# The first layernorm of a two-layer transformer block: statistics first, two tiles normalised on ACT, x loaded on two queues

## The chip, the cores and the metric

The kernel runs on one core of one Trainium2 chip. The metric is the device time of one execution in microseconds (us). A lone core has no second die to compare with, so all timed runs below count as fast ones (the three single looks near the end have the state "unknown"); the granted TensorE clock, the share of full speed that the profiler records, was 0.998 to 1.0 over every whole run.

Engines are named as in the profile: PE is TensorE's matmul side, PEld its weight loads, DVE is VectorE, ACT is ScalarE, POOL is GpSimd, SP is SyncE, which here only issues DMAs.

## The reference

Two layers, each of a dilated sliding-window attention and a dense GELU block, with a layernorm without weights in front of each, over 2048 tokens of width 1024 in bf16:

```python
x = x + A(layernorm(x), wqkv, wo)      # 32 heads of 32; window of 8 keys, dilation 2
x = x + B(layernorm(x), w1, b1, w2, b2) # 1024 -> 3584, gelu, 3584 -> 1024
x = x + A(layernorm(x), wqkv, wo)
x = x + B(layernorm(x), w1, b1, w2, b2)

def layernorm(x):                       # eps 1e-5
    return (x - mean(x)) / sqrt(var(x) + eps)
```

## The kernel before

The kernel works on four groups of 512 tokens, each of four tiles of 128 tokens (`NTT = 4`). All x tiles stay in on-chip memory. What matters here is the head of the program: until the first group's four tiles are normalised, transposed and copied to `xnT`, PE has nothing real to do, because every QKV matmul of a group reads all 512 tokens of `xnT`.

```python
def load_x(g):
    for tt in range(NTT):
        t = g * NTT + tt
        sp.dma_start(x[t][:], x_in[t * P:(t + 1) * P, :])
...
def ln_stats(t):
    stats = lnp.tile([P, 2, 6], F32, name="stats")     # lnp: two buffers of each name
    for h in range(2):
        vec.bn_stats(stats[:, h, :], x[t][:, h * HALF:(h + 1) * HALF])
    mv = lnp.tile([P, 2], F32, name="mv")
    vec.bn_aggr(mv[:], stats[:])
    rstd = lnp.tile([P, 1], F32, name="rstd")
    pool.tensor_tensor(out=rstd[:], in0=mv[:, 1:2], in1=eps_t[:], op=ALU.add)
    pool.tensor_tensor(out=rstd[:], in0=rstd[:], in1=mhalf[:], op=ALU.pow)
    return mv, rstd

def ln_norm(t, mv, rstd):
    xn = lnp.tile([P, D], BF16, name="xn", bufs=3)
    vec.tensor_scalar(out=xn[:], in0=x[t][:], scalar1=mv[:, 0:1], scalar2=rstd[:], op0=ALU.subtract, op1=ALU.mult)
    return xn

def transpose_on_pe(xn, out):
    pst = psum.tile([P, KD, P], BF16, name="acc", bufs=6)
    for k in range(KD):
        pe(nc.tensor.transpose(pst[:, k, :], xn[:, k * P:(k + 1) * P], ident[:]))
    act.copy(out, pst[:])
...
def ln_first():
    ...
    s = [ln_stats(0)]
    for tt in range(NTT):
        if tt + 1 < NTT:
            s.append(ln_stats(tt + 1))
        xn = ln_norm(tt, *s[tt])
        transpose_on_pe(xn, xa[0][:, tt, :, :])
        warm_up(4)                      # four 512-column matmuls on zeros
...
warm_up(16)
ln_first()
build_constants()
...
    load_x(1)
    stage(gen_qkv(0, 2), ...)           # the real work begins
    ...
    stage(q2, 18)                       # Q, K and two of eight V chunks of group 2
    stage(gen_wo(0, 2))                 # then the output projection of group 0
```

In `ln_stats`, mv holds mean and variance of each token, and rstd is one over the standard deviation, which POOL computes from mv in two operations. `warm_up` is there to keep PE active, so that its clock is at full speed when the real matmuls come. A chunk is eight matmuls of PE, 1.73 us. The weights go through one pool of five 1 MB buffers (`wt`), so a weight load waits until PE is done with the tile five loads earlier.

## Time and profile before

| | before |
|---|---|
| median of 3 runs | 1247.13 us (1247.12 to 1247.34) |
| span of the profiled run | 1245.4 us |
| PE busy | 1232.9 us, 99% |
| first QKV matmul starts | 14.18 us |
| PE idle after that, in waits over 0.2 us (named ones) | 0.73, 0.5, 0.5, 0.2 us |

Two lines of the page of before; the first column is the engine's busy time, the second its share of the span:

```profile
PE 1232.9 (99%) x5757; PEld 627.9 (50%) x5807; DVE 836.5 (67%) x863; ACT 305.7 (25%) x475; POOL 97.7 (8%) x215
...
PEclk9999999999999999999999999999999999999999
```

PE is busy for 99% of the span at full clock, so time can be won only where PE does nothing or nothing useful. The timeline of PE in the first 45 us (start in us, duration, engine, line, operation, output and inputs, shapes, count; in brackets the idle time just before and what ended it) shows where that is:

```profile
1.05 4.91 PE L118 MATMUL acc<-big 128*128 128x512 bf16 x16 [1.05 <-DVE big L93]
6.89 0.62 PE L187 MATMUL acc<-ident,xn 128*128 128x128 bf16 x8 [0.93 <-POOL rstd L93]
...
12.37 0.61 PE L187 MATMUL acc<-ident,xn 128*128 128x128 bf16 x8
12.81 1.03 PE L118 MATMUL acc<-big 128*128 128x512 bf16 x4
14.18 26.06 PE L118 MATMUL acc<-xnT,wt 128*128 128x512 bf16 x120 [0.34 <-ACT xnT L93]
```

The matmuls on `big` are warm-up, those on `ident` are the transposes. From 14.18 us on, PE runs real matmuls back to back. DVE in the same stretch (before):

```profile
3.50 1.29 DVE L93 BATCH_NORM_STATS2 stats<-x 128x6 f32<-128x512 bf16 x2 [2.51 <-DMA x<-in_A_x_dram]
4.82 0.21 DVE L93 BATCH_NORM_AGGREGATE mv<-stats 128x2 f32<-128x12 f32 x1
4.95 1.23 DVE L93 BATCH_NORM_STATS2 stats<-x 128x6 f32<-128x512 bf16 x2
...
6.34 0.49 DVE L93 TENSOR_SCALAR xn<-x,mv,rstd 128x1024 bf16<-128x1024 bf16 x1
...
10.50 0.49 DVE L93 TENSOR_SCALAR xn<-x,mv,rstd 128x1024 bf16<-128x1024 bf16 x1
11.70 0.55 DVE L93 TENSOR_SCALAR xn<-x,mv,rstd 128x1024 bf16<-128x1024 bf16 x1 [0.71 <-PE acc L187]
```

DVE starts when the first x tile lands and goes on without a pause until 11.0 us; the last normalisation then waits 0.71 us. It waits for two things, a free `xn` buffer and rstd of its tile, and the line names PE, which reads the buffers.

In the waits of PE between 30 and 200 us (engine and line, what was waited for, us in total, times, longest):

```profile
PE acc L118 <- ACT vT L93: 0.7, 1, 0.7
```

That wait of 0.73 us ends at 100.41 us, where the Q matmuls of group 2 begin.

### The profile page before, as it was taken

What the parts mean: (1) busy time and instruction counts of PE and PEld (TensorE: products, weight loads), DVE (VectorE), ACT (ScalarE), POOL (GpSimd) and SP (SyncE); (2) the same over time, 40 slices, a digit from 0 to 9 for tenths busy, and PEclk for the clock granted to TensorE, in tenths of its full rate; (3) what the DMA queues carried; (4) which work ended last, traced back from release to release, by engine and by line L of the source; (5) the groups of instructions that cost most, each with busy time, mean ns of one, the idle gap of its engine ahead of it and who ended that gap; (6) DMA issues with size and microseconds to landing.
All of it is one profiled execution on the core that took longest, in us unless ns stands there. A gap on an engine that the chain in (4) does not pass through costs nothing.

```text
span 1245.4 us, 13928 instructions
## 1 busy us (share of the span) xinstructions
PE 1232.9 (99%) x5757; PEld 627.9 (50%) x5807; DVE 836.5 (67%) x863; ACT 305.7 (25%) x475; POOL 97.7 (8%) x215
## 2 busy tenths in 40 slices
PE   8999999999999999999999999999999999999998
PEld 5666544446444564445644456444654444444443
DVE  4999989896995999427993379943598786011002
ACT  3333252013430134201341013510234001300310
POOL 3040010012001100101000010000001001000000
PEclk9999999999999999999999999999999999999999
DMA  9755564466846546655556575556654558446441
GB/s 278 262 187 169 153 207 148 161 176 204 215 132 205 167 154 201 191 170 149 177 170 196 166 184 166 162 199 197 182 168 132 186 198 202 157 157 194 156 143 39
DMA packets 215151, 219.81 MB, mean 176 GB/s; under 512 B 66018, under 2 KB 184816, under 8 KB 212016
## 3 DMA queue, kind: packets, MB, share of 16 engines
q1 hardware_dynamic: 212416, 208.16, 55.1%
q0 software_dynamic: 2672, 10.76, 2.6%
q8 instruction: 45, 0.74, 0.2%
q14 instruction: 18, 0.15, 0.0%
HBM read 197.40 MB, written 6.29 MB: 164 GB/s over the span
## 4 chain that ended last, share of the span: by engine, by line
PE 78%; DVE 0%; issue 0%; POOL 0%; DVEq 0%
PE acc L118 78%; PE L L118 0%; DVE x L93 0%; DVE tmp L93 0%; POOL rstd L93 0%; DVE xn L93 0%; DVEq L93 0%
## 5 line engine op out<-in xcount | busy, mean ns | idle before, releaser
L118 PE MATMUL acc<-xnT,wt 128*128 128x512 bf16 x3328 | 722.2, 379 | 1.1 <-ACT vT L93 0.7
L118 PEld LDWEIGHTS <-wt 128*128 128x128 bf16 x3328 | 394.7, 119 | 325.3 <-issue 5.3
L118 PE MATMUL acc<-wt,hT 128*128 128x512 bf16 x1752 | 386.0, 379 | 2.1
L118 PEld LDWEIGHTS <-hT 128*128 128x128 bf16 x1792 | 175.3, 98 | 211.5
L93 DVE TENSOR_TENSOR big<-big 128x2048 bf16<-128x2048 bf16 (+2 forms) x182 | 240.3, 1349 | 1.7
L93 ACT ACTIVATE hT<-acc,b1T 128x512 bf16<-128x512 f32 x224 | 151.7, 687 | 318.3 <-PE acc L118 317.7
L93 DVE TENSOR_TENSOR tmp<-acc,b2bc 128x512 f32<-128x512 f32 x64 | 44.1, 690 | 271.6 <-PE acc L118 267.5
L93 DVE TENSOR_TENSOR big<-abc,vT 128x4096 bf16<-128x4096 bf16 x64 | 144.2, 2282 | 49.3 <-DMA abc<-a_d 49.3
L93 DVE TENSOR_TENSOR big<-qT,kT 128x4096 bf16<-128x4096 bf16 x64 | 143.9, 2286 | 31.4 <-ACT kT L93 30.4
L93 ACT CAST qT<-acc 128x512 bf16<-128x512 f32 x64 | 37.2, 586 | 332.3 <-PE acc L118 332.2
L118 PE MATMUL acc<-wt,oT 128*128 128x512 bf16 x440 | 97.8, 379 | 1.1 <-DVE tmp L93 0.5
L93 DVE BATCH_NORM_STATS2 stats<-x 128x6 f32<-128x512 bf16 x128 | 84.2, 678 | 3.4 <-DMA x<-in_A_x_dram 2.5
L118 PEld LDWEIGHTS <-oT 128*128 128x128 bf16 x448 | 43.9, 98 | 53.9 <-issue 1.5
L93 ACT CAST vT<-acc 128x512 bf16<-128x512 f32 x64 | 37.5, 586 | 84.8 <-PE acc L118 84.8
L93 DVE TENSOR_SCALAR xn<-x,mv,rstd 128x1024 bf16<-128x1024 bf16 x64 | 34.8, 544 | 34.4 <-POOL rstd L93 30.0
L93 POOL TENSOR_TENSOR rstd<-mv,eps_t 128x1 f32<-128x1 f32 x64 | 17.6, 275 | 500.0 <-DVE mv L93 500.0
L93 ACT CAST kT<-acc 128x512 bf16<-128x512 f32 x64 | 37.4, 586 | 70.5 <-PE acc L118 70.5
L93 POOL DMA_DIRECT2D a_d<-a x32 | 19.6, 637 | 412.2 <-DVE a L93 412.2
L93 DVE TENSOR_TENSOR x<-tmp,x 128x512 bf16<-128x512 f32 x64 | 44.1, 690 | 1.8
L93 DVE TENSOR_TENSOR x<-acc,x 128x512 bf16<-128x512 f32 x64 | 42.7, 669 | 2.6 <-PE acc L118 2.3
L93 POOL TENSOR_TENSOR rstd<-rstd,mhalf 128x1 f32<-128x1 f32 x64 | 40.6, 634 | 5.0
L93 DVE TENSOR_TENSOR oT<-big 128x512 bf16<-128x512 bf16 x56 | 22.3, 415 | 0.2
(46 smaller groups left out, 179.4 us busy)
## 6 DMA issues: line engine op xcount, KB each, us to landing
wt<-in_B_w_dram SPq DMA_DIRECT2D x56, 1024.0 KB, 5.6
wt<-in_B_w_dram SPq DMA_DIRECT2D x64, 896.0 KB, 4.8
wt<-in_A_wqkv_dram SPq DMA_DIRECT2D x48, 1024.0 KB, 5.5
wt<-in_A_wo_dram SPq DMA_DIRECT2D x16, 1024.0 KB, 4.9
abc<-a_d POOLq DMA_DIRECT2D x32, 256.0 KB, 4.5
x<-in_A_x_dram SPq DMA_DIRECT2D x16, 256.0 KB, 6.1
out_dram<-x SPq DMA_DIRECT2D x32, 128.0 KB, 1.8
a_d<-a POOLq DMA_DIRECT2D x32, 64.0 KB, 3.6
```

The costliest lines, as they stand in the source:

```text
L93: inst = f(*args, **kwargs)
L118: return pe(nc.tensor.matmul(*args, **kwargs))
```

## The change

The intent: DVE does everything in the first layernorm while ACT idles until 7.5 us. So compute the statistics of all four tiles first, let ACT normalise tiles 0 and 1, let DVE share the copies of the transposed tiles, load x on two queues, and put the loads of group 1 behind the first weights. The names of the statistics need four buffers then, and PE gets six instead of sixteen warm-up matmuls between the transposes.

```diff
-            sp.dma_start(x[t][:], x_in[t * P:(t + 1) * P, :])
+            (act if g == 0 and tt % 2 else sp).dma_start(x[t][:], x_in[t * P:(t + 1) * P, :])
...                                   # zhalo's memset moves to the front, too
-        stats = lnp.tile([P, 2, 6], F32, name="stats")
+        stats = lnp.tile([P, 2, 6], F32, name="stats", bufs=4)
...
-        mv = lnp.tile([P, 2], F32, name="mv")
+        mv = lnp.tile([P, 2], F32, name="mv", bufs=4)
...
-        rstd = lnp.tile([P, 1], F32, name="rstd")
+        rstd = lnp.tile([P, 1], F32, name="rstd", bufs=4)
...
+        if on_act:
+            nmr = lnp.tile([P, 1], F32, name="nmr", bufs=2)
+            pool.tensor_tensor(out=nmr[:], in0=mv[:, 0:1], in1=rstd[:], op=ALU.mult)
+            pool.tensor_scalar(out=nmr[:], in0=nmr[:], scalar1=-1.0, scalar2=None, op0=ALU.mult)
+            act.activation(xn[:], x[t][:], ACT.Identity, bias=nmr[:], scale=rstd[:])
+        else:
+            vec.tensor_scalar(out=xn[:], ...)
...
-        s = [ln_stats(0)]
+        s, xn = [], []
         for tt in range(NTT):
-            if tt + 1 < NTT:
-                s.append(ln_stats(tt + 1))
-            xn = ln_norm(tt, *s[tt])
-            transpose_on_pe(xn, xa[0][:, tt, :, :])
-            warm_up(4)
+            s.append(ln_stats(tt))
+            if tt < 2:
+                xn.append(ln_norm(tt, *s[tt], on_act=True))
+        for tt in range(2, NTT):
+            xn.append(ln_norm(tt, *s[tt]))
+        for tt, copy in enumerate((act.copy, vec.tensor_copy, act.copy, vec.tensor_copy)):
+            transpose_on_pe(xn[tt], xa[0][:, tt, :, :], copy)
+            if tt < 2:
+                warm_up(3)
...
-        load_x(1)
-        stage(gen_qkv(0, 2), sides=at(0, ln_a, 1) + ...
+        stage(gen_qkv(0, 2), sides=at(0, load_x, 1) + at(0, ln_a, 1) + ...
```

The tiles that ACT normalises lie in buffers named `big` (a line left out above), as the zeros of the warm-up do; in the profiles of after, matmuls on `ident,big` are their transposes.

More of the change, by code (lines that the diff above doesn't have):

```diff
@@ L143 @@
     zhalo = const.tile([P, NCH, HALO], BF16, name="zhalo")
+    pool.memset(zhalo[:], 0.0)
     b1T = const.tile([P, KF], F32, name="b1T")
@@ L147, in build_constants @@
     def build_constants():
-        pool.memset(zhalo[:], 0.0)
         pool.memset(smat[:], 1.0)
@@ L177, in ln_stats, with ln_norm, transpose_on_pe @@
         return mv, rstd
-    def ln_norm(t, mv, rstd):
-        xn = lnp.tile([P, D], BF16, name="xn", bufs=3)
-        vec.tensor_scalar(out=xn[:], in0=x[t][:], scalar1=mv[:, 0:1], scalar2=rstd[:], op0=ALU.subtract, op1=ALU.mult)
+    def ln_norm(t, mv, rstd, on_act=False):
+        xn = bigp.tile([P, D], BF16, name="big") if on_act else lnp.tile([P, D], BF16, name="xn", bufs=3)
+        if on_act:
[4 more added lines that the diff above has]
+        else:
+            vec.tensor_scalar(out=xn[:], in0=x[t][:], scalar1=mv[:, 0:1], scalar2=rstd[:], op0=ALU.subtract, op1=ALU.mult)
         return xn
-    def transpose_on_pe(xn, out):
+    def transpose_on_pe(xn, out, copy=act.copy):
         pst = psum.tile([P, KD, P], BF16, name="acc", bufs=6)
@@ L187, in transpose_on_pe @@
             pe(nc.tensor.transpose(pst[:, k, :], xn[:, k * P:(k + 1) * P], ident[:]))
-        act.copy(out, pst[:])
+        copy(out, pst[:])
     late = []
@@ L453 @@
     with tc.tile_pool(name="early", bufs=1) as early:
-        load_x(1)
-        stage(gen_qkv(0, 2), sides=at(0, ln_a, 1) + at(8, load_x, 2) + at(12, load_x, 3) + at(14, load_bias)
+        stage(gen_qkv(0, 2), sides=at(0, load_x, 1) + at(0, ln_a, 1) + at(8, load_x, 2) + at(12, load_x, 3) + at(14, load_bias)
               + at(19, head_sum, 0, False))
```

## The prediction

> **What bounds the kernel now.** The page of before gives TensorE 1232.9 us busy of a 1245.4 us span (99%), clock granted 1.0 throughout. Only the head is open to this change. In the timeline the first real QKV matmul starts at 14.18 us; after that TensorE shows only gaps under 1 us (0.46, 0.73, 0.47, ended by DVE or ACT). So each microsecond off those 14.18 is worth one microsecond.
>
> **The head, from the timeline.** The x tiles land at 3.48, 4.17, 6.45, 7.13 us; the first half of wq at 12.48. DVE runs without a pause from 3.50 to 11.0: per tile two statistics (1.28), aggregate (0.2), normalise (0.49), plus one early statistic of tile 4. It then waits 0.71 us for a free xn buffer. The fourth transpose ends at 12.98, the last two ACT copies (1.01 each) at 14.13, and the matmul starts. wq is not the limit.
>
> **What the change does.** DVE loses two normalisations (2 x 0.41 net), the buffer wait (0.71) and the early statistic (0.6), and gains two copies out of PSUM. GpSimd gains two small operations per ACT tile (about 0.3 us each, as its rstd operations). ACT gains two normalisations; its 128x1024 copy is 1.01, with pointer scale and bias I estimate 1.2. Group 1's loads go behind wq and wk: wq should land near 9.8 instead of 12.5 (four tiles at 0.65 us each leave its path).
>
> Two queues: the Trainium skill, "DMA: Bandwidth & Descriptors", section "Issuing engines are not separate DMA queues", says both interleave on the same 16 engines and save issue time only. The trace agrees in that the tiles land 0.7 us apart though issued 0.47 apart. I expect no earlier tiles; tile 0, now sharing with tile 1, later (3.5 to 4.1), tile 3 near 7.
>
> **New chain (estimate).** Statistics start: tile 0 at 3.9, tile 1 at 5.3, tile 2 at 6.8, tile 3 at 8.1; aggregate ends 9.6. rstd to normalise takes 0.94 (as for tile 4 of before), so tile 3 is normalised from 10.5 to 11.05. DVE is in order: both its copies come after that. Copy of tile 1 to about 11.75, of tile 3 to about 12.5. I take 0.7 us a copy: the Trainium skill, "VectorE: DVE Perf Modes", section "Why PSUM operands drop a tier", lets a 16-bit PSUM source still run two elements per cycle; at one element it is 1.2 and the end about 13.4. No trace here shows it. ACT: normalisations about 6.9 to 9.4, copies of tiles 0 and 2 done by about 12.2. First QKV matmul at about 12.7: 1.4 to 1.5 us saved.
>
> All of it is on the critical path, but it is 0.12% of the run. Group 1's normalisation starts about 10 us later, but DVE idled 7.3 us before its first product (30.54) and its transposes are needed only at about 54.
>
> **Predicted: 1245.7 us, 8 in 10 within 1244.5 to 1247.1.** Chances: faster by over 2% 0.005, within 2% 0.99, slower 0.005.
>
> **What would show it:** x tiles landing at 4 to 7 us; ACT normalising at about 7 and 8 us, 1.2 us each; DVE copies 0.7 us; first QKV matmul at 12.2 to 13.4; that gain kept to the end.
>
> **What would make it wrong.** Warm-up matmuls fall from 16 to 6 after the first sixteen; TensorE idles about 2.4 us from 5.96. If it falls back to its slow spacing (0.43 us per 512-column matmul against 0.22, as in its first microseconds) up to 1.7 us returns. DVE copies at 1.2 us halve the gain. Tiles sharing bandwidth with wq may land later. The second half of wv, now behind two more x tiles, could land late (needed near 41).

## More of the kernel before

The profile's DMA view of the first issue alone says that the first tile landed 2.7 us after its issue at 0.80:

```profile
x<-in_A_x_dram SPq DMA_DIRECT2D x1, 256.0 KB, 2.7
```

## The result

| | before | after |
|---|---|---|
| median of 6 runs | 1247.18 us | 1246.15 us |
| all runs | 1247.01 to 1247.34 | 1246.07, 1246.09, 1246.09, 1246.21; 1247.4, 1247.6 |
| span of the profiled run | 1245.4 us | 1244.4 us |
| first QKV matmul | 14.18 us | 13.69 us |
| Q matmuls of group 2 | 100.41 us | 99.42 us |

The ratio is 0.9995 (95% interval 0.9982 to 1.0008), so by that measure the two are the same. A ratio here is the mean time of one kernel's runs over that of the other's of the same rounds, so not quite the ratio of the medians that are quoted. The interval is far wider than the scatter of the kernel before, whose runs lie within 0.4 us of each other; where every run of one kernel lies below every run of the other, I call half a microsecond a difference.

The median is 1.0 us lower, inside the predicted range. Two readings did not fit the prediction: the head gave only half of that microsecond, and two of six runs were slower than every run of before, and outside the range.

The profile after, in the views that were shown of before. The page:

```profile
PE 1231.1 (99%) x5747; PEld 627.0 (50%) x5797; DVE 837.2 (67%) x863; ACT 306.0 (25%) x475; POOL 98.2 (8%) x219
...
PEclk9999999999999999999999999999999999999999
```

PE, first 32 us:

```profile
1.05 5.34 PE L118 MATMUL acc<-big 128*128 128x512 bf16 x16 [1.05 <-DVE big L93]
9.11 0.62 PE L193 MATMUL acc<-ident,big 128*128 128x128 bf16 x8 [2.72 <-ACT big L93]
...
11.62 1.19 PE L193 MATMUL acc<-ident,xn 128*128 128x128 bf16 x16
13.69 18.54 PE L118 MATMUL acc<-xnT,wt 128*128 128x512 bf16 x85 [0.88 <-DVE xnT L93]
```

DVE:

```profile
4.76 1.29 DVE L93 BATCH_NORM_STATS2 stats<-x 128x6 f32<-128x512 bf16 x2 [3.76 <-DMA x<-in_A_x_dram]
6.08 0.21 DVE L93 BATCH_NORM_AGGREGATE mv<-stats 128x2 f32<-128x12 f32 x1
6.20 1.23 DVE L93 BATCH_NORM_STATS2 stats<-x 128x6 f32<-128x512 bf16 x2
...
10.38 0.49 DVE L93 TENSOR_SCALAR xn<-x,mv,rstd 128x1024 bf16<-128x1024 bf16 x1
11.59 0.55 DVE L93 TENSOR_SCALAR xn<-x,mv,rstd 128x1024 bf16<-128x1024 bf16 x1 [0.71 <-POOL rstd L93]
12.05 1.50 DVE L93 COPY xnT<-acc 128x1024 bf16<-128x1024 bf16 x2
```

The first statistic starts at 4.76 us instead of 3.50. From there on the changed chain needs 13.69 - 4.76 = 8.93 us to the first QKV matmul; the old one needed 14.18 - 3.50 = 10.68. So the change to the chain won 1.75 us, and a late start took 1.26 back. (What each part of the chain contributes, the order of the statistics, ACT's normalisations, DVE's copies, fewer warm-up matmuls, was not tested.) The DMA view of the first two issues, now one on each queue, names the cause of the late start: both tiles landed 3.8 to 3.9 us after their issue at 0.80, where the first tile of before took 2.7.

```profile
x<-in_A_x_dram ACTq DMA_DIRECT2D x1, 256.0 KB, 3.8
x<-in_A_x_dram SPq DMA_DIRECT2D x1, 256.0 KB, 3.9
```

The waits of PE between 30 and 200 us:

```profile
PE acc L118 <- DMA xnT<-xn: 0.2, 1, 0.2
```

The wait before the Q matmuls of group 2 fell from 0.73 to 0.19 us (the line rounds to 0.2). Head and wait together are 0.49 + 0.54 = 1.03 us, which is the whole difference of the spans (1.0). The second half of it was in no step of the prediction.

### The profile page after: what moved, and what is told of

It is laid out like the page before. It is cut to its first block, busy times and chain, and to the rows that moved or that the text cites. A ratio compares the mean times of both kernels' runs of the same rounds, so it can differ in the third digit from the quotient of the medians.

```text
span 1244.4 us, 13914 instructions
## 1 busy us (share of the span) xinstructions
PE 1231.1 (99%) x5747; PEld 627.0 (50%) x5797; DVE 837.2 (67%) x863; ACT 306.0 (25%) x475; POOL 98.2 (8%) x219
## 4 chain that ended last, share of the span: by engine, by line
PE 78%; DVE 0%; issue 0%; POOL 0%; DVEq 0%
PE acc L118 78%; PE L L118 0%; DVE x L93 0%; DVE tmp L93 0%; POOL rstd L93 0%; DVE xn L93 0%; DVEq L93 0%
```

## Experiments

Each kernel was timed in five rounds unless said otherwise, beside runs of the kernel before on the same chip (nine in each of the two batches: 1246.97 to 1247.23, median 1247.09, in the first; 1246.98 to 1247.32, median 1247.24, in the second). All gave correct results.

### One queue for x, the rest of the change kept (e1_one_queue)

```diff
-            (act if g == 0 and tt % 2 else sp).dma_start(x[t][:], ...)
+            sp.dma_start(x[t][:], ...)
```

> The changed kernel with all four first x tiles back on the SP queue, nothing else undone. Theory A (the second queue delays tile 0, and DVE's chain starts with tile 0): the tiles land again near 3.5, 4.2, 6.5 and 7.1 us instead of 4.73, 4.55, 6.00 and 5.58; DVE's first statistic starts near 3.5 instead of 4.76, and the first QKV matmul at 12.4 to 12.9 instead of 13.69; time near 1245.1 us, about 1.0 under the changed kernel's 1246.1. Rival B (tile 0 is late because wq is issued right behind x and shares the engines, whatever the queue): tile 0 stays at 4.5 or later, the matmul starts near 13.7, time 1246.1.

Measured: tile 0 landed at 3.47 us, the first statistic started at 3.50, the first QKV matmul at 12.43. That is Theory A; Rival B is out, for wq is still issued directly behind the x tiles (at 2.66 us; 1.75 in the changed kernel), and in the next experiment tile 0 is late although wq is issued at 4.74, when it has landed. The first statistic and the first QKV matmul of this run:

```profile
3.50 1.29 DVE L93 BATCH_NORM_STATS2 stats<-x 128x6 f32<-128x512 bf16 x2 [2.50 <-DMA x<-in_A_x_dram]
12.43 26.09 PE L118 MATMUL acc<-xnT,wt 128*128 128x512 bf16 x120 [0.88 <-DVE xnT L93]
```

From the first statistic to the matmul it is again 8.93 us. But the time was 1246.08 us, with a scatter the kernel before never has (1245.21, 1245.96, 1246.08, 1246.34, 1247.29). The profiled run (1246.08) shows a wait of PE, between 100 and 200 us, that neither kernel had:

```profile
PE acc L118 <- DMA wt<-in_A_wo_dram: 1.2, 1, 1.2
```

PE was ready for the second half of wo at 130.2 us and got it at 131.35. The load took 6.3 us from issue to landing, against 5.0 in the changed kernel's profile. Its issue waits for a `wt` buffer that PE itself frees some 5.2 us before it needs the load, so the slack was about 0.2 us at most; a load that takes 1.3 us more stalls PE by all of that but the slack. What fell into the load in this run is in the DMA view of 127.5 to 131 us (queue, kind, packets, MB, share):

```profile
q8 instruction: 1, 0.02, 1.7%
```

One 16 KB fetch of instructions. It started at 129.16 us and took 0.98 us; the last packet of wo started at 130.12, where all the others had started by 129.21. In the changed kernel's profile that fetch fell at 125.6, before the load was issued. That the fetch held up one DMA engine and with it the last packet is read from these times, not tested.

### Two queues for x, nothing else of the change (e2_two_queues_alone)

```diff
-            sp.dma_start(x[t][:], ...)
+            (act if g == 0 and tt % 2 else sp).dma_start(x[t][:], ...)      # in the kernel before
```

> The kernel before with only the loads of x tiles 1 and 3 moved to the ACT queue. Theory A: tile 0 lands near 4.7 us instead of 3.48; DVE ran without a pause from tile 0 on, so the first QKV matmul moves from 14.18 to about 15.4 and the time from 1247.15 to about 1248.3. Rival B (the queue does not matter, the wq position does): tile 0 near 3.5, start 14.2, time 1247.15. Rival C (all four tiles in sooner, 6.0 instead of 7.1, is what counts): start 13.5 or earlier, time under 1246.6.

Measured: 1248.16 us (1248.08 to 1248.22), 1.07 us slower than the kernel before, every run slower than every run of it. Tile 0 landed at 4.54, tile 1 at 4.73, tiles 2 and 3 at 5.58 and 5.88; the statistics started at 4.57 instead of 3.50 and the first QKV matmul at 15.25 instead of 14.18:

```profile
4.57 1.29 DVE L93 BATCH_NORM_STATS2 stats<-x 128x6 f32<-128x512 bf16 x2 [3.57 <-DMA x<-in_A_x_dram]
15.25 24.98 PE L118 MATMUL acc<-xnT,wt 128*128 128x512 bf16 x115 [0.34 <-ACT xnT L93]
```

All four tiles were in 1.2 us sooner, and it was worth nothing: DVE takes them in order and has no pause in which it waits for a later one, so only the first arrival counts. Theory A holds, Rivals B and C are out.

### Four buffers of the statistics, nothing else of the change (e3_four_buffers_alone)

```diff
-        stats = lnp.tile([P, 2, 6], F32, name="stats")
+        stats = lnp.tile([P, 2, 6], F32, name="stats", bufs=4)              # likewise mv and rstd, in the kernel before
```

> The kernel before with only four buffers instead of two for stats, mv and rstd. Theory A (half of the measured gain is not in the head at all, but at the start of the third group's Q matmuls near 100 us, where the transposed xnT landed 1.0 us sooner because two aggregates no longer wait for a free mv and rstd buffer): head unchanged at 14.18 us, TensorE's wait near 100 us falls from 0.73 to 0.3 us or less, time 1246.55 to 1246.75. Rival B (that wait shrank because the head moved everything): wait stays 0.7, time 1247.15.

Measured: 1246.55 us (1246.44 to 1246.62), 0.54 us faster than the kernel before, every run faster than every run of it. The head did not move to the better (14.33 us in this run, its first tile landing at 3.63); the wait near 100 us fell from 0.73 to 0.18. DVE from 91.5 us, first in the kernel before, then with four buffers:

```profile
91.77 1.16 DVE L93 TENSOR_SCALAR xn<-x,mv,rstd 128x1024 bf16<-128x1024 bf16 x2
92.85 0.33 DVE L93 BATCH_NORM_AGGREGATE mv<-stats 128x2 f32<-128x12 f32 x2
93.98 0.55 DVE L93 TENSOR_SCALAR xn<-x,mv,rstd 128x1024 bf16<-128x1024 bf16 x1 [0.81 <-POOL rstd L93]
94.44 2.28 DVE L93 TENSOR_TENSOR big<-abc,vT 128x4096 bf16<-128x4096 bf16 x1
96.65 0.55 DVE L93 TENSOR_SCALAR xn<-x,mv,rstd 128x1024 bf16<-128x1024 bf16 x1
```

```profile
92.07 1.61 DVE L93 TENSOR_SCALAR xn<-x,mv,rstd 128x1024 bf16<-128x1024 bf16 x3
93.60 2.29 DVE L93 TENSOR_TENSOR big<-abc,vT 128x4096 bf16<-128x4096 bf16 x1
96.02 0.55 DVE L93 TENSOR_SCALAR xn<-x,mv,rstd 128x1024 bf16<-128x1024 bf16 x1
```

In the kernel before, two aggregates stand behind the first two normalisations, because with two buffers of mv and rstd they may not write until those have read; then DVE waits 0.81 us for rstd, and the fourth normalisation starts at 96.65. With four buffers these two aggregates ran at 75.5 and 78.3 us, three normalisations follow each other, and the fourth starts at 96.02 though this run was 0.15 us late. The transposing DMA behind it took 3.1 us in the kernel before (issued at 97.22, landed at 100.28), and the Q matmuls of group 2 started at 100.41. The profile of before put that wait down to an ACT copy (of vT); it was the DMA, as the lines of after and of this run name it: in all three runs the Q matmuls start 0.13 to 0.14 us after that DMA lands, and in after and in this run they start before the vT copy has ended.

### The changed kernel with two buffers in all later layernorms (e5_two_buffers_later)

```diff
+        nb = 4 if own else 2                                  # own = "_first" in the first layernorm
...                                                            # stats: back to two buffers
-        mv = lnp.tile([P, 2], F32, name="mv", bufs=4)
+        mv = lnp.tile([P, 2], F32, name="mv" + own, bufs=nb)  # rstd: as mv
```

A first form, with own buffers for stats as well, did not build for want of on-chip memory.

> The changed kernel with its four buffers of mv and rstd kept for the first layernorm alone; every later layernorm has two buffers of stats, mv and rstd as in the kernel before. Theory A: first QKV matmul at 13.7 us as in the changed kernel, but TensorE's wait near 100 us is back at about 0.7 us, time about 1246.6 (the fast ones of its runs). Rival B: wait stays 0.2, time 1246.1.

Measured: 1246.47 us (1246.39 to 1246.62). First QKV matmul at 13.60, wait near 100 us back at 0.74. So the head is worth 0.6 us and the buffers 0.5, and each acts without the other: 0.62 + 0.54 = 1.16 us for the two alone, against 1.0 to 1.4 together (1247.18 - 1246.15 above, 1247.24 - 1245.81 below).

### The long runs: first attempts (e9_after_again, e4_more_warm_up, e7_later_wo)

Two of the first six runs of the changed kernel were 1.4 us over the others. After the run with one queue there were two theories. Theory W: the second half of wo lands late, as seen there. Theory C: PE's clock falls back, as the prediction feared.

The changed kernel again:

> The changed kernel once more, unaltered, as the neighbour of the next three runs on one chip. Two of its first six runs were 1.3 to 1.5 us over the rest (1247.6 and 1247.4 against 1246.1). Both theories of that expect one or more of five runs near 1247.4 again and the others near 1246.1. If the profiled run is a long one, theory W (the second half of wo near 131 us) expects TensorE to wait over 1 us for that load, theory C (cold clock) expects 512-column matmuls 0.43 us apart after the head.

Measured: 1245.81 us; 1245.71, 1245.72, 1245.81, 1246.26 and one of 1246.95. The profiled run was a short one, with the matmul at 13.39 us. Nothing decided.

Ten more warm-up matmuls at the start:

```diff
     warm_up(16)
+    warm_up(10)                                  # in the changed kernel
```

> The changed kernel with 26 instead of 16 warm-up matmuls at the start, which fill most of TensorE's idle stretch before the first transposes (2.7 us in the changed kernel). Theory C (the long runs are those in which the array falls back to its slow spacing in that stretch): no run over 1246.4, all near 1246.1. Theory W: long runs still occur, or vanish only by chance; head unchanged at 13.6 to 13.8 us.

Measured: 1245.97 us (1245.62 to 1246.19), no long run. The first QKV matmul of the profiled run started at 13.30 us, sooner than the 13.6 to 13.8 expected; its tile 0 had landed at 4.36.

The output projection of group 0 one V chunk later:

```diff
-        stage(q2, 18)                            # in the changed kernel
+        stage(q2, 19)
         stage(gen_wo(0, 2))
-        stage(q2, sides=... + at(3, head_sum, 1, False) + at(4, transpose_late))
+        stage(q2, sides=... + at(2, head_sum, 1, False) + at(3, transpose_late))
```

> The changed kernel with the first output projection (wo of group 0) one V chunk of TensorE work (1.73 us) later, so that the second half of wo has that much more time to land after its buffer came free. Theory W (the long runs wait for that load, when a 16 KB instruction fetch shares one of its DMA engines): all five runs at 1246.0 to 1246.3, none near 1247.4, and no wait on wo in the profile. Theory C: the long runs stay.

Measured: 1245.74 us (1245.65 to 1246.13), no long run either; the 1246.13 is the profiled run, whose tile 0 landed at 4.91 and whose first QKV matmul started at 13.86. Each of the two theories had predicted the end of the long runs in its own experiment, and none came in either (four of these five runs were even faster than the range given). With three long runs of eleven by then, five short ones in a row come by chance in one case out of five ((8/11)^5 = 0.20), so series of five could not settle this. A profile of a long run could.

### Looks at the changed kernel (e10a_after_look, e10b_after_look, e10c_after_look)

The changed kernel without any edit, three single profiled runs.

> The changed kernel unaltered, one profiled run, to catch one of its long runs (3 of 11 so far). If it is short (1245.7 to 1246.3): no wait over 0.3 us on wo near 130 us. If it is long (1246.9 to 1247.6): theory W expects a wait of 1.0 to 1.4 us on the second half of wo, landing over 6 us after its issue instead of 5.0, with an instruction fetch inside that time; theory C expects the first QKV matmuls 0.43 us apart and no wait on wo.

> A second look at the unaltered changed kernel, for the same purpose and with the same expectations: short run, no wait on wo; long run, theory W a wait of 1.0 to 1.4 us on the second half of wo, theory C slow matmuls after the head.

> A third look at the unaltered changed kernel, same purpose and expectations: short run, no wait on wo; long run, theory W a wait of 1.0 to 1.4 us on the second half of wo, theory C slow matmuls after the head.

Measured: 1247.48, 1245.86 and 1247.11 us: two long, one short. In both long runs the second half of wo landed 5.0 us after its issue and PE did not wait for it. Theory W falls for these long runs. Theory C stands, though not quite as I had put it: not the first QKV matmuls were slow, but the transposes and warm-up matmuls just before them. PE in the first long run, then in the short one:

```profile
1.05 4.96 PE L118 MATMUL acc<-big 128*128 128x512 bf16 x16 [1.05 <-DVE big L93]
8.95 0.62 PE L193 MATMUL acc<-ident,big 128*128 128x128 bf16 x8 [2.94 <-ACT big L93]
...
10.96 1.49 PE L118 MATMUL acc<-big 128*128 128x512 bf16 x3
12.24 1.91 PE L193 MATMUL acc<-ident,xn 128*128 128x128 bf16 x16
15.03 11.20 PE L118 MATMUL acc<-xnT,wt 128*128 128x512 bf16 x51 [0.88 <-DVE xnT L93]
```

```profile
1.05 5.63 PE L118 MATMUL acc<-big 128*128 128x512 bf16 x16 [1.05 <-DVE big L93]
8.95 0.62 PE L193 MATMUL acc<-ident,big 128*128 128x128 bf16 x8 [2.27 <-ACT big L93]
...
10.81 0.81 PE L118 MATMUL acc<-big 128*128 128x512 bf16 x3
11.46 1.19 PE L193 MATMUL acc<-ident,xn 128*128 128x128 bf16 x16
13.52 12.71 PE L118 MATMUL acc<-xnT,wt 128*128 128x512 bf16 x58 [0.88 <-DVE xnT L93]
```

Three warm-up matmuls took 1.49 instead of 0.81 us and sixteen transposes 1.91 instead of 1.19. The table of windows (stretch, length, busy time and count of PE, PEld, DVE, ACT, POOL, then the granted clock, DMA share and GB/s) has the reason, again long run first:

```profile
10.00:12.00 2.00, 1.87 (x12) 1.06 (x12) 1.25 (x5) 1.19 (x2) 1.48 (x4) 0.65 1.05 388
12.00:14.00 2.00, 2.00 (x18) 1.64 (x15) 0.56 (x1) 0.66 (x1) 0.77 (x11) 0.50 1.05 387
```

```profile
10.00:12.00 2.00, 1.86 (x21) 1.19 (x19) 1.25 (x5) 1.20 (x2) 1.47 (x4) 1.00 1.04 385
12.00:14.00 2.00, 1.12 (x13) 0.82 (x12) 1.26 (x2) 1.01 (x1) 0.78 (x11) 1.00 1.04 386
```

The granted clock fell to half. The trace's clock record has it at 0.5 from 10.62 to 14.03 us in the first long run and from 9.12 to 12.53 in the other, 3.41 us each; in the short one it stays at 1.0 once it has risen at 5.15 us. PE had idled 2.94 us there before its first transpose (2.00 in the other long run, 2.27 in the short one). The slow stretch pushes PE's transposes, and with them DVE's last copies, back: the first QKV matmul starts at 15.03 (14.75 in the other), which is 1.51 and 1.23 us after the short run's 13.52, and the runs are 1.62 and 1.25 us longer. All three profiled runs had tile 0 at 4.56 to 4.58 us, so the arrival of x is not the difference. None of the 25 runs of the kernel before was long.

That leaves the other three long runs (1247.6, 1247.4 and 1246.95), of which there is no profile; they have about the same size, and I take them to be the same, but that is not shown. And it leaves two reasons for a long run in two kernels: in the kernel with one queue, where PE idled 1.73 us, the profiled run shows full clock and the wait for wo.

### One queue, and the output projection one V chunk later (e6_one_queue_later_wo)

The edits of e1_one_queue and e7_later_wo together, on the changed kernel.

> The changed kernel with all x loads on the SP queue and the first output projection one V chunk later. In the run with one queue alone the first QKV matmul started at 12.43 us, 1.75 before the kernel before, but TensorE then waited 1.21 us for the second half of wo. Theory W: that wait goes, the head's gain reaches the end, time 1244.7 to 1245.0 in all runs (1247.1 less 1.75 in the head and about 0.6 near 100 us). Rival G (another wait in the DVE-bound stretch to 260 us gives the gain back): 1245.5 to 1246.2, with a new wait in the profile.

Measured: 1244.84 us (1244.74, 1244.82, 1244.84, 1244.95, 1245.03), against 1247.24 of the kernel before and 1245.81 of the changed kernel in the same batch; ratio 0.9981 (0.9969 to 0.9994). The first QKV matmul started at 12.49 us, wo was not waited for, and every run was shorter than every run of both kernels. The gain of the head, 14.18 - 12.49 = 1.69 us, and of the wait near 100 us, 0.73 - 0.15 = 0.58, sum to 2.27, which is the difference of the spans (1245.4 - 1243.1 = 2.3). So the expectation from Theory W held for this variant, and Rival G is out. In the profiled run the fetch ended at 126.0 us, just before the first packet of wo, and the load took 5.0 us; what a fetch inside the load costs with the new slack is not seen. This is the best version found, 2.4 us (0.2%) under the kernel before. It still has the idle stretch on PE before the first transpose (0.42 us in this run, 1.73 in the profile of e1_one_queue, the difference being how late PE's first matmuls came up to speed: the clock rose at 6.80 us here, at 4.02 there), and five runs do not show that its clock never falls back.

## Why the prediction was right, and where it was not

The predicted time was 1245.7 us in a range of 1244.5 to 1247.1; the median was 1246.15, and 1245.81 in the later batch. "Within 2%" was never in doubt, since the head is 1% of the run. The sum was right partly by luck: two errors had opposite signs, a head that gained 0.49 us where 1.4 to 1.5 were expected, and 0.54 us at 100 us that were not expected at all.

1. **"Only the head is open to this change": wrong.** The change also gave every later layernorm four buffers, and 0.54 us of the gain comes from there, at 100 us (e3_four_buffers_alone has it without the head, e5_two_buffers_later takes it away alone). I had listed the 0.73 us wait, believed the ACT label of it, and not asked what `bufs=4` does outside the first layernorm, although the order of DVE's instructions near 75 and 92 us was there to compare.
2. **"Statistics start: tile 0 at 3.9": the term that was mis-sized.** Tile 0 landed at 4.73 (range given: 3.5 to 4.1) and the statistic started at 4.76. This 0.86 us is most of the difference between the predicted 12.7 us and the measured 13.69 of the first QKV matmul; e1_one_queue and e2_two_queues_alone show 1.26 and 1.07 us for the second queue from either side. I had counted the sharing of bandwidth. With perfect sharing both tiles would have landed when the second one did before, at 4.17; tile 0 came 0.2 to 0.7 us later still, in all runs with two queues that I profiled (4.36 to 4.91). In the trace fewer packets move early: by 2.5 us 28 and 23 had started in the changed kernel and in e2_two_queues_alone, 64 and 58 in the kernel before and in e1_one_queue. What delays them stays open. A second queue also means that all four tiles are issued by 1.26 us instead of 2.19, and no run separates the queue from the earlier issue. (Nor do the tiles of before land evenly "0.7 us apart", as the prediction has it: between tiles 1 and 2 lie 2.28 us.)
3. **The chain from the first statistic: right in its length, wrong in one link.** Predicted 12.7 - 3.9 = 8.8 us, measured 8.93 in the changed kernel and in e1_one_queue. But DVE did not lose "the buffer wait (0.71)": the same 0.71 us stand before the last normalisation of the changed kernel, where no buffer is short, now put down to POOL's rstd. That wait had been rstd all along; the estimate came out right because it had the 0.94 us from aggregate to normalise in it. ACT's normalisations took 1.24 us (predicted 1.2), DVE's two copies 1.50 together (predicted 0.7 each). The Trainium skill, "VectorE: DVE Perf Modes", section "Why PSUM operands drop a tier", allows two elements per cycle from a 16-bit PSUM source, and 0.75 us for 1024 elements agrees: by an estimate from the clock of 0.96 GHz that the page's section "Specifications" gives, at one element per cycle the elements alone would take 1.07 us.
4. **"I expect no earlier tiles": wrong for tiles 2 and 3** (6.00 and 5.58 instead of 6.45 and 7.13), but without effect, as e2_two_queues_alone shows. In e1_one_queue, on one queue, they also landed earlier than before (5.67 and 6.49).
5. **"If it falls back to its slow spacing ... up to 1.7 us returns": right as a risk, and it does happen.** It costs 1.2 to 1.6 us and is what two profiled long runs show. Five of fourteen runs of the changed kernel were long. The predicted idle time of 2.4 us was 2.72 in the first profiled run; with tile 0 in time it is 1.73 (e1_one_queue).
6. **"The second half of wv ... could land late": did not happen.** It landed at 40.27 us (37.48 before), and PE did not wait for it. The load with no slack was another, the second half of wo near 131 us, which the change does not touch; it showed in one profile alone, that of e1_one_queue, where the head is shorter and a fetch of instructions fell into the load.

## What to carry to other kernels

Where a chain starts with the first of several loads and works on them in order, a second queue can cost time although all loads are in sooner: look at when the first one lands, not the last. A buffer count is a property of every use of the name; compare the order of instructions in all stages, not only in the one meant. When some runs are longer by about the same amount, profile a long run before explaining it: here two good theories each passed their own test, and the profiles of two long runs decided.

## What the Trainium skill lacked or had wrong

- "TensorE: Matmul & The Clock Gate", section "What's actually happening", has the array fall back to half clock after at least one idle window of about 3.4 us. Here it fell back after idle gaps of 2.94 and 2.00 us, so a wholly idle window was not needed; a gap of 2.27 us in a third run did not do it. The half-clock stretches of 3.41 us agree with the page. That the length of the gap alone does not decide agrees with its remark that the window is free-running. In the 3.41 us before the clock fell, ordinary matmuls had run for 0.81 and 1.26 us; the page gives no share below which a window counts as idle. With the transposes PE was busy for 1.54 and 1.41 us of these windows; counted from the clock's rise in steps of 3.41 us, windows with 1.52 and 1.53 us (e5_two_buffers_later, e7_later_wo, e10b_after_look) left the clock at full speed, so these runs give no limit of busy time either.
- "DMA: Bandwidth & Descriptors", section "Issuing engines are not separate DMA queues", says that issuing from several engines saves the sequencer's time only. It does not say that this can lose: with the four first tiles on two queues tile 0 took 3.6 to 4.1 us from issue to landing in all profiled runs, instead of 2.7 to 2.8 on one queue, and e2_two_queues_alone was 1.07 us slower.
- "Runtime: NRT & Kernel Launch", section "Instruction fetch mechanics", has each sequencer fetch its instructions in 16 KiB blocks through a DMA queue of its own and calls the cost "mostly hidden". The traces agree on the size (45 packets, 0.74 MB on the instruction queue) and show about 1 us for most packets. What the page lacks is that such a fetch can coincide with a data load that has no slack: in e1_one_queue the wo load with a fetch inside it took 6.3 instead of 5.0 us, and PE waited 1.21 us.
